# A fused attention and feed-forward kernel: a new order, new buffer slots and new queues for all its instructions, and the query norms of one batch taken from a product

## The chip, the cores and the metric

The kernel runs on one core of one Trainium2 chip. A core has a matrix engine (TensorE, PE in the profile; its weight loads are the row PEld), VectorE (DVE), ScalarE (ACT), GpSimd (POOL) and SyncE (SP). They run side by side, each through its own instructions in order, and wait for each other by semaphores. DMAs are issued from the instruction streams of SP and ACT and share 16 DMA engines. The metric is the device time of one execution in microseconds, as the median of several runs. TensorE's clock is granted at one of two levels, 1.2 or 2.4 GHz; the profile gives the mean granted share.

## The reference

For 8 batches and 8 heads of width 64 there are 512 local positions and 32 global ones. Global queries see everything; a local query sees the 32 global keys and the local keys at most 32 positions away. The result of the attention, 4352 rows of 512, goes through a feed-forward part with a smooth activation:

```
s_g   = scale * q_g @ concat(k_g, k_l).T ;  out_g = softmax(s_g) @ concat(v_g, v_l)
s_ll  = where(|i - j| <= 32, scale * q_l @ k_l.T, -1e9)
out_l = softmax(concat(scale * q_l @ k_g.T, s_ll)) @ concat(v_g, v_l)
x     = concat(out_g, out_l) as (4352, 512)
h     = x @ w_in                                   # 512 -> 2048
g     = h if h >= 1, 0 if h <= -1, else (h+1)^2/4
out   = g @ w_out                                  # 2048 -> 512
```

## The kernel before

Values are kept as pairs of 16-bit numbers, a high part and the remainder (`split`, `halves`), so that a product is made of three 16-bit products. Before a tensor is split it is scaled by a power of two taken from its norm. The weights arrive as 64-bit numbers and are decoded on the chip in the first part of the run.

The work is cut into named steps, about 900 of them. For batch b: `Lk`, `Lq`, `Lv` load keys, queries and values from the input; `sk`, `sq`, `sv` find their scales; `pk`, `pq`, `pv` split tile by tile and, for keys and queries, turn the tile (`turn`: by TensorE and a copy in batch 0, by a transposing DMA afterwards); `sw` and `vw` copy turned queries and shifted values within the on-chip memory by DMA; `aq` makes the local scores, `aa` their softmax and its turn, `ab` the product with the values, `ax` the normalised result, its split and its turn into the operand of the feed-forward part; `ga` and `gb` are the global queries. For the weights: `Lw`, `wd`, `ws`, `wh` load, decode, scale and split w_in; `Lo`, `od`, `oh` do so for w_out; `cb` and `rp` form sums of weight blocks. The feed-forward part works on tiles of 256 rows, s = 0 to 15: `m` is the first product with the activation (`moe1` for tiles 0 and 1, `moe_f`, a seven-product form that also uses the sums of blocks, afterwards), `o` the second product and the store.

`scale_q` finds the scale of a batch's queries: in batch 0 in two calls (`sq0a` for query tiles 0 and 1, `sq0b` for tiles 2, 3 and the global queries), later in one. With `gramq` "a" each tile's squares are summed by one ScalarE instruction (`squares`); with "p" the tiles are multiplied with themselves on TensorE (`gram`), VectorE sums the diagonal, and one small product adds that over the partitions (`total`, `all_sum`).

What is done is written by `attention_moe`; when it is issued is written out by hand. `segments` (line numbers below) cuts every step into stretches, the instructions of one step that run on one engine without an inner dependence, and numbers them in the order of the steps. `ORDER` is a list of these numbers. `build` records the instructions twice and issues the stretches in that order, so each engine runs its own stretches as `ORDER` has them. `SLOTS` says which of the fixed buffers each new tile takes (38 of 2 KB per partition called "room", 6 called "twin", 8 PSUM banks, and small ones). `T["queues"]` says for each plain load or copy in turn whether SP ("s") or ACT ("a") issues it; a load issued by SP also waits for the fifth SP load before it (`AHEAD`). Transposing DMAs are all issued by SP. Other letters in `T` choose the engine of one kind of instruction: `casts` and `subs` for the two halves of a softmax tile, `glow` for the remainder of an activation tile, `lows` and `lowx` for the remainder of an attention result, `turns` for the copy behind a turn by TensorE in batch 0 (a ScalarE, v VectorE, p GpSimd).

Every instruction is issued from line 1348 and every DMA from lines 1351 and 1353, so the profile's groups are told apart by tiles: "room", "bank" (PSUM), "twin", "weights_w" and small ones.

Of the kernel before, what the change touches and what calls it, by code (L numbers as in the profile page):

```python
# [118 lines left out]
def plan(steps, tiles):  # L119

    sizes, line = segments(steps, tiles)
    order = [int(x) for x in ORDER.split()]
    assert sorted(order) == list(range(len(sizes)))
# [8 lines left out]
def attention_moe(nc, memory, q_l, k_l, v_l, q_g, k_g, v_g, w_in, w_out, out):  # L132
# [1137 lines left out]
    for _, _, fn, a in sorted(steps.values(), key=lambda x: x[:2]):  # L1270
# [8 lines left out]

SLOTS = {  # L1280
# [27 lines left out]
}  # L1308

T = dict(es="nnnn", gramq="aaaaaaaa", dg="vvvvvvaaaaavvav", sid="vvvvv", fast=2, grams="ppaaaaaa", sqs="maamaa", cb=200, cbs=5, lk0=4.19,  # L1310
         lq0=1.76, lv0=12, sk=12, sq=14, subs="ppppppvppvppvpppppppvpvppvppvppppvvvvvpppvppvppppvpppvvvpppvpvpp",
         glow="ppppvvpppvpppvppppvvppvppvpvvppvpppppvpvppvpppvvppppvvvppvvpvvvpppvpvvpvppppvppvppvpvpvpppppppvvpvpppppvppppvvvvpvppvpvvpppvppvvpppppppppppppppp",
         turns="aaaaaaaaaaavvvvvvvvaaaa", casts="aaaaaavvaaaavvvvvvvaavavaaavvvaaavvaaaaaavaavvvvvaaaavvaavavaaav",
         mags="aapapvpaappvppppppapapaaaaapaaaa", lowx="ppppppppvpvvpppvppppppvpvpppvpvvvppvvpvppppvpvpp",
         lows="ppppvpppppppvpppppvpvpppvpppvpvp", halves="aaaaaahaabacadacceccacdbidffcbdf", shifts="vavvaaavvvvaaavvvvvavvvvvaaavvvv",
         splits="wpvpwwpvwwvpvvvw", att=1.35, s0=60, s1=100, s2=254.09, wd0=4, wds=2.06, wd8=19.2, wdt=1.9, wh=1.5, whs=1.4, od=58.2,
         ods=2.2, oh=0.7, ohs=0.92, e0=25.78, e1=70, e2=120, e3=156, w0=24.7, w1=24.34, w2=25.15, w3=25.51, z1=18.29, lq1=24, lv2=24.36,
         sv=24.5, sqb=35.02, pk2=20.4, pk3=30, pk4=45.8, pq2=28.03, pq4=44, pv=35.24, pvs=0.33, lw=0.54, lo=32.46, los=2.12, mk=8, mks=2,
         queues="saasasaaassaassaaaaasassaaaaaaassasaaaasasaasassasasssasssasssasssssasssaasssssssaaaaasassaaaasassssssaaaaaassasaasaassasaasasssssssssaasssassssssasssaasssssassaasaaaasassasasssaasssssaaassasssssaasassaasssaassasssssassasaassasasaasssaaaasasaasasssssasaassaaasssssasasaasaassaaasssasssssaaaasssssaassssssaassaaaasaasasaaaaassssasasssaassassassaassaaaassasaassssssaasasssssasasassaasaaasssaaaassassaasssasssaassassassssasassaasasasasaassaasssassasssssaasasaaaasssaasssssaassasassasaassssaassassasasassaaassssssassasaaaaasssaassasasassasaassssasasassaassssaasasaaasassaasssasass")
# [70 lines left out]
```

## Time and profile before

| | |
|---|---|
| median of 3 runs | 925.06 us (923.33 to 927.4) |
| the profiled execution | 925.07 us |
| its span (first to last instruction) | 923.0 us |
| TensorE busy, share of the span | 845.0 us, 92% |
| VectorE busy | 744.2 us, 81% |
| ScalarE busy | 643.9 us, 70% |
| GpSimd busy | 311.1 us, 34% |
| mean granted clock of TensorE | 0.993 |

A busy time is the union of an engine's instructions, so it takes in waits between matmuls that overlap in their pipeline. The idle time of an engine is put down to the engine or DMA that released it. Idle time costs only where that engine is the one all others wait for.

### The profile page before, as it was taken

The numbers are of one execution on the slowest core, as the hardware profiler recorded it, in microseconds if no ns is written. First come the engines' busy times: TensorE is split into PE (matmuls) and PEld (weight loads), VectorE is DVE, ScalarE is ACT, GpSimd is POOL, SyncE is SP. The second block draws the span as 40 slices with busy tenths as digits, with TensorE's granted clock in tenths as the row PEclk, the third lists the DMA queues.
The fourth block names the chain that finished last, engine by engine and source line by source line (L and its number), as shares of the span: only waits on it lengthen the run. The fifth ranks groups of instructions, "written<-read, shape, count | busy, mean of one in ns | idle before, by whom it ended". The sixth has DMA issues, their size and how long they took to land.

```text
span 923.0 us, 34948 instructions
## 1 busy us (share of the span) xinstructions
PE 845.0 (92%) x14380; PEld 613.3 (66%) x14380; DVE 744.2 (81%) x2008; ACT 643.9 (70%) x1592; POOL 311.1 (34%) x350
## 2 busy tenths in 40 slices
PE   1487889999999999899899998999999999999998
PEld 1354787557866766767586857668677768686953
DVE  3889999998889986799878888787979859867661
ACT  2698797878768877578668776778588658654530
POOL 3425354614232333232413212422435052324140
PEclk9989999999999999999999999999999999999999
DMA  9988896599989999999997979999987894772101
GB/s 237 243 219 202 190 187 116 121 198 165 177 150 179 175 171 164 155 173 167 166 178 110 163 163 172 163 151 192 178 160 139 159 147 90 129 128 36 26 19 51
DMA packets 379711, 140.96 MB, mean 153 GB/s; under 512 B 348576, under 2 KB 357792, under 8 KB 379552
## 3 DMA queue, kind: packets, MB, share of 16 engines
q1 hardware_dynamic: 305968, 98.94, 64.8%
q10 hardware_dynamic: 73584, 39.80, 19.0%
q8 instruction: 112, 1.84, 0.9%
q14 instruction: 47, 0.39, 0.2%
HBM read 49.81 MB, written 8.91 MB: 64 GB/s over the span
## 4 chain that ended last, share of the span: by engine, by line
PE 48%; DVE 19%; DMA 17%; ACT 7%; issue 4%; POOL 2%; ACTq 1%; SPq 1%; DVEq 0%; POOLq 0%
PE bank L1348 48%; DVE room L1348 11%; DMA room<-room 8%; ACT room L1348 5%; DVE bank L1348 3%; POOL room L1348 2%; DMA room<-in_q_l_dram 2%; DMA room<-in_v_g_dram 2%; DMA weights_w<-in_moe_w_in_dram 1%; DVE weights_w L1348 1%; ACT junk_junka L1348 1%; DMA room<-in_k_g_dram 1%; ACTq L1351 1%; DMA out_dram<-room 1%; DMA pg_gpt<-const_pgb 1%
## 5 line engine op out<-in xcount | busy, mean ns | idle before, releaser
L1348 POOL TENSOR_TENSOR room<-room,room 128x512 f16<-128x512 f32 (+3 forms) x228 | 245.8, 1090 | 505.8 <-ACT room L1348 379.9
L1348 PEld LDWEIGHTS <-room 128*32 128x32 f16 (+3 forms) x7560 | 249.4, 97 | 238.8 <-issue 33.5
L1348 PE MATMUL bank<-weights_w,room 128*128 128x512 f16 x1632 | 367.5, 379 | 3.5 <-issue 1.1
L1348 PEld LDWEIGHTS <-weights_w 128*128 128x128 f16 (+1 forms) x3968 | 220.1, 98 | 32.4 <-DVE weights_w L1348 13.9
L1348 PE MATMUL bank<-room,weights_w 128*128 128x128 f16 (+1 forms) x3840 | 221.4, 216 | 8.5 <-ACT room L1348 2.6
L1348 ACT CAST room<-room 128x512 f16<-128x512 f32 (+1 forms) x245 | 140.2, 587 | 69.9 <-DVE room L1348 48.4
L1348 PE MATMUL bank<-room,twin 128*128 128x128 f16 (+1 forms) x2304 | 132.6, 217 | 9.2 <-DMA room<-room 6.4
L1348 PEld LDWEIGHTS <-twin 128*128 128x128 f16 x2304 | 125.5, 98 | 16.1 <-DMA room<-room 7.3
L1348 ACT ACTIVATE room<-room,small_nb 128x128 f32<-128x128 f32 x256 | 100.6, 394 | 26.5 <-DVE small_nb L1348 21.7
L1348 ACT ACTIVATE room<-bank,batch_small_ms 128x512 f32<-128x512 f32 (+1 forms) x112 | 83.1, 749 | 31.6 <-DVE bank L1348 11.9
L1348 DVE SCALAR_TENSOR_TENSOR bank<-bank,batch_small_ms,room 128x512 f32<-128x512 f32 (+1 forms) x112 | 80.3, 722 | 21.8 <-ACT room L1348 21.7
L1348 ACT ACTIVATE junk_junka<-room 128x512 f16<-128x512 f32 (+2 forms) x124 | 77.4, 624 | 25.6 <-DMA room<-in_q_l_dram 6.7
L1348 ACT COPY room<-bank 128x512 f32<-128x512 f32 (+2 forms) x104 | 60.1, 585 | 41.8 <-PE bank L1348 38.9
L1348 DVE TENSOR_TENSOR room<-room,room 128x512 f16<-128x512 f32 (+1 forms) x90 | 69.8, 779 | 16.9 <-ACT room L1348 16.5
L1348 DVE CUSTOM_DVE_ANT_0 room<-bank,const_mask,batch_small_q 128x128 f32<-128x128 f32 x256 | 74.0, 345 | 7.4 <-PE bank L1348 4.3
L1348 DVE SCALAR_TENSOR_TENSOR room<-room,batch_small_ms,bank 128x512 f32<-128x512 f32 (+1 forms) x112 | 78.8, 712 | 1.0
L1348 DVE TENSOR_TENSOR bank<-bank,room 128x512 f32<-128x512 f32 (+1 forms) x64 | 42.0, 659 | 19.9 <-PE bank L1348 16.1
L1348 DVE SCALAR_TENSOR_TENSOR room<-room,batch_small_ms,room 128x512 f32<-128x512 f32 (+1 forms) x64 | 49.5, 775 | 6.1 <-ACT room L1348 5.8
L1348 ACT ACTIVATION_READ_ACCUMULATOR room<-room,small_nb 128x1 f32 x256 | 48.3, 189 | 0.0
L1348 DVE TENSOR_SCALAR room<-bank,batch_small_ms 128x512 f32<-128x512 f32 x34 | 25.3, 745 | 25.3 <-PE bank L1348 24.6
L1348 DVE SCALAR_TENSOR_TENSOR room<-room,batch_small_sk,room 128x512 f16<-128x512 f32 (+1 forms) x46 | 37.9, 829 | 5.3 <-ACT room L1348 4.1
L1348 PE MATMUL bank<-keys_kt,room 128*32 128x128 f16 x2048 | 37.8, 223 | 2.6 <-DMA room<-room 1.8
(168 smaller groups left out, 893.1 us busy)
## 6 DMA issues: line engine op xcount, KB each, us to landing
room<-room SPq DMA_DIRECT2D x87, 128.0 KB, 4.4
room<-room ACTq DMA_DIRECT2D x57, 128.0 KB, 4.2
weights_w<-in_moe_w_in_dram ACTq DMA_DIRECT2D x21, 256.0 KB, 5.2
room<-in_q_l_dram SPq DMA_DIRECT2D x20, 256.0 KB, 5.3
twin<-in_moe_w_out_dram ACTq DMA_DIRECT2D x17, 256.0 KB, 4.8
out_dram<-room SPq DMA_DIRECT2D x17, 256.0 KB, 4.3
room<-in_v_l_dram SPq DMA_DIRECT2D x22, 192.0 KB, 3.8
room<-in_k_l_dram SPq DMA_DIRECT2D x21, 192.0 KB, 4.8
```

Source lines behind the costliest of these rows:

```text
L1348: getattr(getattr(tc.nc, engine), op)(*a, **k)
L1351: r = (tc.nc.scalar if queue[n] == "a" else tc.nc.sync).dma_start(*a)
```

## The change

- All stretches are put in a new order, and all buffers get new slots. `ORDER` has 4417 numbers in place of 4411.
- Of the 576 letters of `queues`, 293 differ (s 323, a 253 become s 326, a 250).
- Engines: `subs` 31 letters differ (VectorE's share 20 becomes 23), `glow` 63 (48 becomes 49), `casts` 27 (27 becomes 30), `lowx` 15 (15 becomes 16), `lows` 9 (7 becomes 8), `turns` 12 (8 stays 8).
- `gramq` is "p" for batch 0: its query norms come from `total`. The code of `total` was there and unused.
- The small tile lists change to match (`small.tr` is new, `small.asx` has 16 entries in place of 14).

The function that takes another path, unchanged in text:

```
    def total(o, tiles, name):
        t = gram(tiles, f"gr{name}")
        tr = sm.tile([P, 1], F32, tag="tr", name=f"tr{name}")
        nc.vector.tensor_tensor_reduce(out=t, in0=t, in1=ident, scale=1.0, scalar=0.0, op0=ALU.mult, op1=ALU.add, accum_out=tr)
        all_sum(o, tr, name)
```

The diff, cut: the first numbers of each long list, and the letters that the prediction speaks of.

```diff
-ORDER = ("9 8 61 62 63 40 193 64 0 298 66 41 38 39 3 29 27 37 30 28 33 32 34 31 2 76 77 78 79 80 81 82 83 84
...
+ORDER = ("12 13 3 2 99 100 101 102 103 0 85 66 47 46 211 304 58 185 5 231 29 212 305 186 306 299 104 307 308 300
...
 SLOTS = {
-    "room": "11 12 4 3 6 5 2 1 0 28 34 11 22 13 10 15 20 29 17 33 14 19 23 36 31 37 24 20 26 16 21 32 25 16 17
...
+    "room": "0 1 18 5 13 19 14 7 24 1 22 9 23 9 32 11 17 21 21 36 34 35 10 2 26 25 29 19 32 3 6 31 28 2 3 16 5
...
+    "small.tr": "0 0",
+    "small.asx": "0 0 1 1 0 1 0 1 1 0 1 0 1 0 1 0",
...
-T = dict(es="nnnn", gramq="aaaaaaaa", dg="vvvvvvaaaaavvav", sid="vvvvv", fast=2, grams="ppaaaaaa", sqs="maamaa", cb=200, cbs=5, lk0=4.19,
+T = dict(es="nnnn", gramq="paaaaaaa", dg="vvvvvvaaaaavvav", sid="vvvvv", fast=2, grams="ppaaaaaa", sqs="maamaa", cb=200, cbs=5, lk0=4.19,
...
-         turns="aaaaaaaaaaavvvvvvvvaaaa", casts="aaaaaavvaaaavvvvvvvaavavaaavvvaaavvaaaaaavaavvvvvaaaavvaavavaaav",
+         turns="aaavavvvvaaaaavaaavavaa", casts="avaaaaavaavaavavvvavvavaavaavavavvaaaaaaavvvavvvavvaaavvvvavavav",
...
```

(In `turns` the letters stand for key tiles 0 to 5, query tiles 0 to 4, the eight softmax tiles and the four results of batch 0.)

## Rows read from the trace of the kernel before

**Rows 1.** The page's first part: busy us (share), count, of each engine.

```profile
PE 845.0 (92%) x14380; PEld 613.3 (66%) x14380; DVE 744.2 (81%) x2008; ACT 643.9 (70%) x1592; POOL 311.1 (34%) x350
```

**Rows 2.** Busy time by stage: start:end length, engines, granted clock, DMA share, GB/s.

```profile
0.00:46.14 46.14, 14.02 (x196) 11.62 (x197) 28.12 (x67) 20.48 (x37) 19.77 (x51) 1.00 1.06 240
46.14:207.63 161.49, 142.42 (x2361) 103.53 (x2361) 153.26 (x455) 135.23 (x334) 68.25 (x67) 0.97 0.83 176
207.63:899.73 692.10, 669.64 (x11755) 489.77 (x11743) 559.68 (x1485) 487.61 (x1224) 223.12 (x232) 1.00 0.86 145
899.73:923.00 23.27, 18.87 (x88) 8.35 (x86) 3.15 (x5) 0.62 (x1) 0.00 (x0) 1.00 0.16 53
```

**Rows 3.** TensorE's waits in 207.63 to 899.73: us, times, longest.

```profile
PE bank L1348 <- DMA room<-room: 12.8, 11, 3.8
PE bank L1348 <- DVE room L1348: 3.3, 5, 1.2
```

**Rows 4.** Timeline of the start: us, duration, engine, instruction, count, idle before it.

```profile
10.49 1.04 PE L1348 MATMUL bank<-room 128*128 128x128 bf16 x8 [10.49 <-DMA room<-in_k_l_dram]
13.54 1.86 PE L1348 MATMUL bank<-room 128*128 128x128 bf16 x16 [2.02 <-DMA room<-in_k_g_dram]
...
15.44 0.29 DVE L1348 TENSOR_REDUCE small_amk<-bank 128x1 f32<-128x128 f32 x1 [7.86 <-PE bank L1348]
...
17.34 0.16 DVE L1348 RECIPROCAL batch_small_sk<-batch_small_sk 128x1 f32<-128x1 f32 x1
...
19.72 1.11 POOL L1348 TENSOR_SCALAR room<-room,batch_small_sk 128x512 f32<-128x512 f32 x1
...
40.69 1.04 PE L1348 MATMUL bank<-keys_kt,room 128*32 128x128 f16 x32
```

**Rows 5.** Groups by shape, whole run: count, busy us, mean ns, idle before.

```profile
L1348 POOL TENSOR_TENSOR room<-room,room 128x512 f16<-128x512 f32 x157 | 192.3, 1236 | 432.9 <-ACT room L1348 329.3 <-DVE room L1348 35.8 <-DMA room<-room 19.7
...
L1348 ACT CAST room<-room 128x512 f16<-128x512 f32 x215 | 129.3, 613 | 64.2 <-DVE room L1348 43.0 <-PE bank L1348 4.2 <-DMA room<-room 4.1
...
L1348 DVE TENSOR_TENSOR room<-room,room 128x512 f16<-128x512 f32 x85 | 67.0, 793 | 15.5 <-ACT room L1348 15.1
L1348 ACT ACTIVATE junk_junka<-room 128x512 f16<-128x512 f32 x102 | 63.7, 624 | 18.9 <-DMA room<-in_q_l_dram 6.7 <-DMA room<-in_k_g_dram 5.0 <-DMA room<-in_k_l_dram 2.3
...
L1348 ACT ACTIVATION_READ_ACCUMULATOR junk_junka<-room 128x1 f32 x102 | 19.2, 188 | 0.0
...
L1348 POOL TENSOR_TENSOR room<-room,room 128x256 f16<-128x256 f32 x25 | 18.4, 745 | 63.8 <-ACT room L1348 50.6 <-DVE room L1348 13.3
...
L1348 DVE CAST room<-room 128x512 f16<-128x512 f32 x27 | 12.6, 469 | 5.3 <-ACT room L1348 5.0
```

**Rows 6.** Groups by shape in 46.14 to 207.63: the copies behind turns.

```profile
L1348 DVE COPY room<-bank 128x1024 f16<-128x1024 f16 x8 | 5.3, 679 | 0.0
...
L1348 ACT COPY room<-bank 128x1024 f16<-128x1024 f16 x6 | 5.9, 990 | 0.0
```

**Rows 7.** DMA issues: engine, kind, count, KB each, median us to landing.

```profile
room<-room SPq DMA_DIRECT2D x87, 128.0 KB, 4.4
...
room<-room SPq DMA_TRANSPOSE x140, 4.4
```

**Rows 8.** TensorE's timeline: three of its waits for DMAs.

```profile
374.88 5.46 PE L1348 MATMUL bank<-room,twin 128*128 128x128 f16 x72 [3.83 <-DMA room<-room]
441.65 1.92 PE L1348 MATMUL bank<-keys_kt,room 128*32 128x128 f16 x124 [1.79 <-DMA room<-room]
453.12 0.55 PE L1348 MATMUL bank<-room,room 128*32 128x64 f16 x48 [1.59 <-DMA room<-room]
```

**Rows 9.** TensorE by stretch behind the first of them: busy, granted clock, DMA share, GB/s.

```profile
374.00:376.00 2.00, 1.12 (x11) 0.54 1.28 146
376.00:378.00 2.00, 2.00 (x25) 0.61 0.76 223
378.00:380.00 2.00, 2.00 (x39) 1.00 0.57 129
```

**Rows 10.** Timeline of the end: last products, last VectorE instruction.

```profile
889.73 28.87 PE L1348 MATMUL bank<-weights_w,room 128*128 128x512 f16 x133
...
918.64 0.75 DVE L1348 TENSOR_SCALAR room<-bank,batch_small_ms 128x512 f32<-128x512 f32 x1 [1.84 <-PE bank L1348]
```

**Rows 11.** TensorE's timeline: one run of short products, for their spacing.

```profile
446.10 1.50 PE L1348 MATMUL bank<-room,weights_w 128*128 128x128 f16 x24
```

More of the change, by code (lines that the diff above doesn't have):

```diff
@@ L1308 @@
 }
-T = dict(es="nnnn", gramq="aaaaaaaa", dg="vvvvvvaaaaavvav", sid="vvvvv", fast=2, grams="ppaaaaaa", sqs="maamaa", cb=200, cbs=5, lk0=4.19,
-         lq0=1.76, lv0=12, sk=12, sq=14, subs="ppppppvppvppvpppppppvpvppvppvppppvvvvvpppvppvppppvpppvvvpppvpvpp",
-         glow="ppppvvpppvpppvppppvvppvppvpvvppvpppppvpvppvpppvvppppvvvppvvpvvvpppvpvvpvppppvppvppvpvpvpppppppvvpvpppppvppppvvvvpvppvpvvpppvppvvpppppppppppppppp",
-         turns="aaaaaaaaaaavvvvvvvvaaaa", casts="aaaaaavvaaaavvvvvvvaavavaaavvvaaavvaaaaaavaavvvvvaaaavvaavavaaav",
-         mags="aapapvpaappvppppppapapaaaaapaaaa", lowx="ppppppppvpvvpppvppppppvpvpppvpvvvppvvpvppppvpvpp",
-         lows="ppppvpppppppvpppppvpvpppvpppvpvp", halves="aaaaaahaabacadacceccacdbidffcbdf", shifts="vavvaaavvvvaaavvvvvavvvvvaaavvvv",
+T = dict(es="nnnn", gramq="paaaaaaa", dg="vvvvvvaaaaavvav", sid="vvvvv", fast=2, grams="ppaaaaaa", sqs="maamaa", cb=200, cbs=5, lk0=4.19,
+         lq0=1.76, lv0=12, sk=12, sq=14, subs="vpppppppvpppvvppvpppvvpvpvvppvppppvppppvvvvvpvvpppppvpppppvppvpv",
+         glow="ppppvppppvppppppvppvpvpvpvppppvvvpvppvpppvppppvpvpvpppvvpppvppvvvpppvvvpvvpvppvppppppvppppvvpvppvpvvvppvppppvppvvpvppvvpppvpvvvvpppppppppppppppp",
+         turns="aaavavvvvaaaaavaaavavaa", casts="avaaaaavaavaavavvvavvavaavaavavavvaaaaaaavvvavvvavvaaavvvvavavav",
+         mags="aapapvpaappvppppppapapaaaaapaaaa", lowx="ppppppppvpppvvvvpppvppvpvpppvpppvpvvpvppvpvvpppp",
+         lows="vpppppppvpppvpppvpppppvpppvpvpvp", halves="aaaaaahaabacadacceccacdbidffcbdf", shifts="vavvaaavvvvaaavvvvvavvvvvaaavvvv",
          splits="wpvpwwpvwwvpvvvw", att=1.35, s0=60, s1=100, s2=254.09, wd0=4, wds=2.06, wd8=19.2, wdt=1.9, wh=1.5, whs=1.4, od=58.2,
@@ L1318 @@
          sv=24.5, sqb=35.02, pk2=20.4, pk3=30, pk4=45.8, pq2=28.03, pq4=44, pv=35.24, pvs=0.33, lw=0.54, lo=32.46, los=2.12, mk=8, mks=2,
-         queues="saasasaaassaassaaaaasassaaaaaaassasaaaasasaasassasasssasssasssasssssasssaasssssssaaaaasassaaaasassssssaaaaaassasaasaassasaasasssssssssaasssassssssasssaasssssassaasaaaasassasasssaasssssaaassasssssaasassaasssaassasssssassasaassasasaasssaaaasasaasasssssasaassaaasssssasasaasaassaaasssasssssaaaasssssaassssssaassaaaasaasasaaaaassssasasssaassassassaassaaaassasaassssssaasasssssasasassaasaaasssaaaassassaasssasssaassassassssasassaasasasasaassaasssassasssssaasasaaaasssaasssssaassasassasaassssaassassasasassaaassssssassasaaaaasssaassasasassasaassssasasassaassssaasasaaasassaasssasass")
+         queues="asassssasssaaaaaaassasasasasasaasaaaassasaassssssssasaaassssssssaaaaasassasssssaasssassaasssasassssssassasasasssasassaasasassaaassaassssaasaasaasasaasaasssssssasssssassssaasaasssassasasssassassssaassasssaassssasassassasasassasasaaasassasssasaaaaaasaaaaaassaassasaasasaasassaaasssaaaasasasassssasasasassssassaaasaaaaaaaassssssssaasaaasasasassaasssassaasssssaassssssaassasaasssaaaaasssaaassassssassasssaaaassaasssasaasasassasaasaaasaassassssassaaasasssssaassssssaaasssssassssssasasssssssssaassssaaaasssasssaaaaaaaasssassassasasasassssssssasasssassaasaasaasasassaaasasassssaaaass")
 KEYS = 2
```

2 lines of the change are left out of this document (1 added, 1 removed), and 21 rows, old and new, of the table SLOTS.

## The prediction, made before the change was timed

> **What bounds the kernel now.** I read the page's busy times first: TensorE is busy for 92% of the span, no other engine for more than 81% [rows 1]. An average over 923 us says little, so the table by stage comes next [rows 2]. It shows three regimes. In the first 46.14 us TensorE works 14.0 us and the DMA engines are full (share 1.06, 240 GB/s): the start waits for data. From 46.14 to 207.63 TensorE works 142.4 of 161.5 us while VectorE works 153.3, or 95%; there VectorE is the tightest. From 207.63 to 899.73 TensorE is busy 669.6 of 692.1 us and VectorE only 81%; TensorE is the bound and idles 22.5 us in all. The last 23 us are its final products and the store. Idle TensorE is all that a new order can give back: 32.1 + 19.1 + 22.5 + 4.4 = 78 us, of which the first term hangs on the loads and the last on the final store.
>
> The waits of TensorE in the third stage come third: 12.8 of the 22.5 us are for DMAs within the chip (turned or shifted tiles), 11 times, the longest 3.8 us [rows 3]. Three single ones show where [rows 8]; the longest also costs clock: behind it the granted share is 0.54 and 0.61 for two windows of 2 us and then 1.00 again [rows 9], that is (0.46 + 0.39) x 2 = 1.7 us at half clock.
>
> The sum is made against the profiled execution, 925.07 us, of which 2.07 lie outside the span; the median of the runs shown is 925.06, so nothing has to be shifted.
>
> **How the two orders can be compared without running them.** `ORDER` numbers stretches of named steps. Step times, and so the numbering, are the same in both versions but for the norms: in `sq0a` and again in `sq0b`, `total` has five stretches where two squares stood, so a new number is the old one up to `sq0a`, 3 more behind it and 6 more behind `sq0b` (4411 + 6 = 4417, as the lists have it). So every number has a name on either side, and I can count what stands ahead of what. Where I weigh a distance, a 128x512 product counts 0.22 us (133 in 28.87 us [rows 10]) and a 128x128 one 0.06 us (24 in 1.50 us [rows 11]), and a VectorE instruction the mean of its kind. These are distances within an order, not times.
>
> **Part 1, the norms by a product.** Removed: four squares on ScalarE, each 0.624 + 0.188 us [rows 5], 3.2 us. Added: 16 small products (eight take 1.04 us [rows 4]) and two single ones, 2.1 us of TensorE; and on VectorE two sums over a diagonal, two casts and two copies, about 2 x 0.29 + 4 x 0.16 = 1.2 us by the nearest rows [rows 4]. TensorE runs nothing before 10.49 us and is idle two thirds of the first stage, so the products cost 0 while they stay there; if they had to queue behind other work they would cost their 2.1 us. ScalarE's 3.2 us are worth 0 in that stage too (20.5 of 46.1 us busy).
>
> **Part 2, the start.** Queries now load first, weights between, and the last piece of batch 0's keys is issued behind 6.1 MB of loads; before, behind 2.0 MB. The keys' products started by 13.54 us [rows 4], so 2.0 MB took 11.7 us (174 GB/s); at the stage's 240 GB/s 6.1 MB take 25.4 us from 1.8 us on, which puts the last keys at 27 us. From there the shortest chain to the first scores is: products 1.9 and the scale's small operations 2.1 (15.44 to 17.50), then key tile 1 by GpSimd (1.11 scaling, 0.61 cast, 1.24 subtraction), turn 8 x 0.06, copy 0.99 [rows 4 to 6, 11]: 8.5 us, so the first scores could start at 35.5 us. They start at 40.69 us now [rows 4]. So the late keys need not delay anything. VectorE is the check: 31.1 us of its work stood ahead of the fourth score product, 34.4 us stand there now, but of that 15.2 us are placed ahead of the key norms where 2.2 us were, and can be done while the keys load. Later the two orders need the same VectorE work per TensorE work (138.2 and 138.7 us ahead of the point where TensorE has done 80 us, 203.3 and 201.0 at 150). I take 0 for the loads, with bounds of -5.2 (scores at 35.5) and +4.7 (keys at 174 GB/s: 35 + 1.8 + 8.5 = 45.4).
>
> **Part 3, the engine letters in the second stage.** VectorE copied all eight softmax turns of batch 0 there, 0.679 us each [rows 6]; now two, and one of the results' turns: -4.1 + 0.7. The five other copies moved to VectorE are of the keys and queries, in the first stage, where it idles. `glow` of tiles 0 to 3 goes from 11 to 9 on VectorE (-1.6 at 0.793 [rows 5]), `lowx` of tile 3 from 2 to 0 (-1.0, half size, taken as 0.5 each), `casts` of batch 1 from 4 to 3 (-0.5), `subs` of batch 1 from 2 to 3 (+0.8). Sum -5.7 us of 153.3. ScalarE takes five copies of 0.99 and a cast of 0.6; it has 26 us free there. How much of 5.7 arrives depends on whether VectorE's waits fill again; bounds -5.7 and 0, and I take -3. Over the whole run, by the same means (three whole `subs`, one `glow`, one `lows`, half a `lowx`, three `casts`), VectorE gains 5.9 + 1.2 us of work, nothing where it is 81% busy and TensorE the bound; with that cover gone it would be up to 5.9 us.
>
> One thing could turn this part round. Four subtractions go from VectorE to GpSimd (two whole, two of half size). If VectorE had to stand still while GpSimd runs them, they would cost it 2 x 1.24 + 2 x 0.75 = 4.0 us [rows 5] where I credit 2.6; the part would come to -5.7 + 2.6 + 4.0 = +0.9, halved as above +0.5, and the sum 3.5 us later. In the stage the two were recorded busy for 153.3 + 68.3 us of 161.5 [rows 2], so at least 60 us overlap; a blocked span may count as busy, so this does not settle it, and I keep the 3.5 us as a rival. The Trainium skill, "SBUF — State Buffer", section "SBUF: two separate sides", states such a rule: GpSimd and a VectorE instruction with two on-chip inputs shut each other out for the whole instruction. By that rule the sum is 922.5, by the overlap of the rows 919; I go by the rows.
>
> **Part 4, the steady stage.** A DMA lands 4.4 us after issue [rows 7]. Of the transposing DMAs placed beyond 150 us of TensorE work, 30 had their first product less than 4.4 us of TensorE work behind them; in the new order 20. Of the copies 14; now 19. Together 44 become 39. Below 3 us it is 26 against 27. So the slack is wider for the turns, not for the copies, and by the counts 5/44 of 12.8 + 1.7 us goes, 1.6 us. By place: the 3.83 us wait (tile 5's sums behind the turn of batch 2's last result) had 2.8 to 3.8 us and gets 8.1 to 9.5; the 1.59 us wait (last quarter of batch 3) 8.1, now 12.0; the 1.79 us wait (queries 1 of batch 4) 2.7, now 0, which may grow to 4.4 [rows 8]. That is -3.8 - 1.7 - 1.6 + 2.6 = -4.5. I take -3, between the two, with bounds of -14.5 (all of it) and +8.8 (two new full landings). Changed queue letters I price at 0: both queues stay as full (326 and 250 against 323 and 253).
>
> **Part 5, the end.** The last products are again those of tiles 14 and 15, followed by a VectorE instruction and a store [rows 10]: 0, bounds -1 and +2 (two more stores wait near the end).
>
> Sum: 925.07 + 0 + 0 - 3 - 3 + 0 = 919.
>
> **Rivals.** (a) *No change*: what the wider turns give, the closer copies take, and VectorE's 5.7 us refill: 925. For it: 26 against 27 below 3 us. Against it: the longest wait is one that gets wider. (b) *Slower, by the keys*: they load at 174 GB/s behind 6.1 MB, first scores at 45.4 us in place of 40.69, and since VectorE is 95% busy behind that nothing is made up; the two sw/vw hand-overs at 0 distance add up to 2.6: 925 + 4.7 + 2.6 = 932. It decides from keys later than 40.69 - 8.5 = 32.2 us, or below 200 GB/s. For it: the same kind of load had 174. Against: the stage's mean is 240, and queries are ready earlier. (c) *Much faster*: all of part 3, all DMA waits of the steady stage: 925 - 5.7 - 14.5 = 905. For it: slack at the places where it waited. Against: the unchanged counts. (d) *GpSimd holds VectorE*: 922.5, by 60 us of overlap unlikely to cost it all.
>
> **Chances.** The forecast (913 to 920) 0.35, (c) 0.15, (a) 0.22, (d) 0.05, (b) 0.23. What a measurement of this kernel can tell from no change is about 0.5%, 4.6 us: faster is below 920.4, 0.35 + 0.15 = 0.50; same 0.22 + 0.05 = 0.27; slower, above 929.7, 0.23. The range runs from 905, the end of (c), to 931, just short of (b), and leaves 0.1 on either side; the likeliest case alone spans 913 to 920.
>
> **What would show it.** Right: key products at about 27 us and first scores by 41; VectorE's busy time in 46 to 207 us down by 3 to 6 us with TensorE's up; the DMA waits of the steady stage near 10 us with none at tile 5's sums. Wrong: first scores beyond 45 us (b); a new wait of 3 us or more with a clock near 0.5 behind it; VectorE spans longer beside GpSimd's (d). The forecast fails as a whole if the third stage's idle time changes by more than 9 us either way.

## The result and the profile after

The changed kernel takes 917.75 us as the median of 20 runs, against 927.98 us for the kernel before, measured beside it in 20 runs. The ratio is 0.9892, with a 95% interval of 0.9861 to 0.9922: 1.1% faster, some 10 us. The forecast was 919.0 us, a ratio of 0.9934 on its own base of 925.07.

The first profiled execution of the changed kernel (924.27 us) was granted less clock than any other run of it (mean 0.971), so what follows is read from a second profiled execution, of 912.69 us; its span is 911.0 us.

The page's busy times after; the row before is [rows 1]:

```profile
PE 843.1 (93%) x14398; PEld 612.4 (67%) x14398; DVE 737.5 (81%) x2025; ACT 638.0 (70%) x1581; POOL 300.0 (33%) x344
```

TensorE's span is its busy time and its idle time. Before, 923.0 = 845.0 + 78.0; after, 911.0 = 843.1 + 67.9. So 10.1 of the 12.0 us between the two executions (their medians differ by 10) are idle time that is gone; the other 1.9 us are busy time, although the change adds 18 products. Where the idle time went is in the table by stage, with the second and the third stage cut once more. First the kernel before, then the changed one (columns as in [rows 2]):

```profile
46.14:102.00 55.86, 46.10 (x726) 30.58 (x725) 52.89 (x181) 50.20 (x132) 21.73 (x25) 0.91 0.82 206
102.00:207.63 105.63, 96.32 (x1639) 72.95 (x1638) 100.37 (x275) 85.02 (x203) 46.51 (x42) 1.00 0.83 161
207.63:420.00 212.37, 203.66 (x3544) 147.83 (x3532) 177.90 (x486) 159.34 (x404) 72.73 (x76) 0.99 1.04 167
420.00:899.73 479.73, 465.98 (x8215) 341.94 (x8212) 381.78 (x1000) 328.27 (x821) 150.39 (x156) 1.00 0.78 135
```

```profile
0.00:46.14 46.14, 17.50 (x174) 14.18 (x175) 30.51 (x69) 16.40 (x25) 17.95 (x49) 0.85 1.05 228
46.14:102.00 55.86, 40.72 (x717) 26.29 (x715) 53.07 (x189) 49.55 (x133) 17.62 (x21) 0.91 0.95 223
102.00:207.63 105.63, 103.57 (x1808) 78.90 (x1806) 98.14 (x288) 89.41 (x214) 55.21 (x55) 1.00 0.91 166
207.63:420.00 212.37, 207.51 (x3602) 153.79 (x3600) 182.67 (x494) 166.93 (x419) 63.72 (x65) 1.00 1.00 169
420.00:899.73 479.73, 466.47 (x8078) 336.09 (x8076) 370.18 (x984) 315.71 (x792) 145.54 (x155) 1.00 0.79 132
899.73:911.00 11.27, 7.33 (x34) 3.14 (x32) 2.91 (x4) 0.00 (x0) 0.00 (x0) 0.95 0.31 118
```

Length less TensorE's busy time is its idle time:

| us of the span | idle before | idle after | difference |
|---|---|---|---|
| 0 to 46.14 | 32.1 | 28.6 | -3.5 |
| 46.14 to 102 | 9.8 | 15.1 | +5.4 |
| 102 to 207.63 | 9.3 | 2.1 | -7.3 |
| 207.63 to 420 | 8.7 | 4.9 | -3.9 |
| 420 to 899.73 | 13.8 | 13.3 | -0.5 |
| the end | 4.4 | 3.9 | -0.5 |

The gain stands in two places: between 102 and 207.63 us, where TensorE now hardly waits at all, and between 207.63 and 420 us. The first row is not a gain of its own: of the 3.5 us by which TensorE is busier there, 2.8 are the new norm products. From 46 to 102 us the changed kernel even waits more; its first scores come later (44.16 against 40.69 us, below). Behind 420 us the two run alike.

TensorE's waits from 207.63 to 899.73 us after (columns as in [rows 3]):

```profile
PE bank L1349 <- issue: 7.4, 5, 2.5
PE bank L1349 <- DVE room L1349: 5.8, 8, 2.3
PE bank L1349 <- DMA room<-room: 2.7, 4, 0.8
```

The 12.8 us for on-chip DMAs have become 2.7, and the longest 0.8. Other traces bear this out: the first profile of the changed kernel has 3.4 us of them and run 7, with the same order, 4.4, while runs 4 and 6 with the old order have 15.0 and 12.1. Against these 10.1 us stand 7.8 of others: waits for VectorE's tiles went from 3.3 to 5.8 us, and gaps that the trace gives no reason for ("issue") from 2.1 to 7.4. Whether it is the same time passed on is not shown; run 4, whose time does not differ from the kernel before's, has 9.4 us of such gaps. The stage's idle time is down by 4.4 us, from 22.5 to 18.1.

The start of the changed kernel, by the timeline (columns as in [rows 4]):

```profile
26.09 2.83 PE L1349 MATMUL bank<-room 128*128 128x128 bf16 x24
...
30.53 0.28 DVE L1349 TENSOR_REDUCE small_amk<-bank 128x1 f32<-128x128 f32 x1
...
33.97 0.15 DVE L1349 RECIPROCAL batch_small_sk<-batch_small_sk 128x1 f32<-128x1 f32 x1
...
37.81 4.02 DVE L1349 SCALAR_TENSOR_TENSOR room<-room,batch_small_sk,room 128x512 f16<-128x512 f32 x3
38.42 1.01 ACT L1349 COPY keys_kt<-bank 128x1024 f16<-128x1024 f16 x1 [0.40 <-PE bank L1349]
...
44.16 1.04 PE L1349 MATMUL bank<-keys_kt,room 128*32 128x128 f16 x32
```

The keys' products start at 26.09 us, and the first scores at 44.16, where they started at 40.69 before [rows 4].

### The profile page after: what moved, and what is told of

It reads as the page before. It is cut to its first block, busy times and chain, and to the rows that moved or that the text cites. A ratio compares the mean times of both kernels' runs of the same rounds, so it can differ in the third digit from the quotient of the medians.

```text
span 922.5 us, 35007 instructions
## 1 busy us (share of the span) xinstructions
PE 851.5 (92%) x14398; PEld 619.4 (67%) x14398; DVE 738.2 (80%) x2025; ACT 638.8 (69%) x1581; POOL 300.5 (33%) x344
## 4 chain that ended last, share of the span: by engine, by line
PE 53%; ACT 4%; DVE 4%; DMA 3%; issue 2%; ACTq 0%; POOL 0%; SPq 0%; DVEq 0%
PE bank L1349 53%; ACT room L1349 3%; DVE room L1349 3%; DMA room<-room 2%; ACT junk_junka L1349 1%; DMA keys_kt<-room 1%; DMA room<-in_k_g_dram 0%; DVE batch_small_q L1349 0%; DMA room<-in_v_g_dram 0%; ACT const_gpf L1349 0%; DVE bank L1349 0%; ACTq L1352 0%; POOL room L1349 0%; DVE batch_small_ms L1349 0%; DVE const_pgb L1349 0%
## 5 line engine op out<-in xcount | busy, mean ns | idle before, releaser
L1349 PEld LDWEIGHTS <-room 128*32 128x32 f16 (+3 forms) x7576 | 254.4, 99 | 240.7 <-issue 38.4
L1349 POOL TENSOR_TENSOR room<-room,room 128x512 f16<-128x512 f32 (+3 forms) x222 | 234.9, 1068 | 531.4 <-ACT room L1349 387.4
L1349 ACT ACTIVATE junk_junka<-room 128x512 f16<-128x512 f32 (+2 forms) x120 | 75.1, 626 | 13.3 <-DMA room<-in_v_g_dram 4.6
L1349 ACT COPY room<-bank 128x512 f32<-128x512 f32 (+2 forms) x106 | 62.6, 595 | 31.3 <-PE bank L1349 24.3
L1349 DVE SCALAR_TENSOR_TENSOR room<-room,batch_small_sv,room 128x512 f16<-128x512 f32 (+1 forms) x47 | 38.8, 832 | 4.8 <-ACT room L1349 4.5
```

What stands on the lines that cost most here:

```text
L1349: getattr(getattr(tc.nc, engine), op)(*a, **k)
```

## The experiments

My theory (theory 1 in the expectations) was the prediction's: the second stage gains because VectorE is relieved, the steady stage because products stand farther behind the DMAs that feed them, and each gives a few microseconds on its own. The rivals put all of the gain in one of the two stages, or say that order, letters and buffers are worth something only together. "Planned" buffers are those that `SLOTS` of the kernel before or of the changed one lists for its own order. Each run was timed in five rounds beside the kernel before; ratios below 1 are faster than that kernel.

**1. The changed kernel again.** No edit.

> The changed kernel once more, for a second profile. All theories: ratio to the kernel before 0.986 to 0.992, as measured. In its profile, theory 1 (mine: both the VectorE-bound second stage and the steady stage give a few us each) expects TensorE's waits for on-chip DMAs beyond 207.63 us near 10 us against 12.8 before. Theory 2 (the steady stage gives all) expects them under 4 us and idle TensorE beyond 207.63 us below 15 us against 22.5. Theory 3 (the first 207 us give all) expects TensorE to be ahead by some 10 us of work at 207 us.

Measured: 0.9869 (0.9813 to 0.9925). The DMA waits are 2.7 us, as theory 2 (all from the steady stage) had them, but the idle time beyond 207.63 us is 22.1 us with the end's, against 26.9: less than 5 us. At 207.63 us TensorE had done the same scores as before and, beyond them, 12 products of 128x512, 96 of 128x64 and 11 of 128x256. At 0.22 us [rows 10], 0.01 (96 of them take 0.98 us) and 0.11 (half of a 128x512) that is 4.8 us ahead. So of 12.0 us in these two executions some 5 were there by 207.63 us and some 7 came behind: theory 1's split at twice its sizes, though not its DMA waits near 10 us. The split is rough. In the first profile of the changed kernel TensorE was 1.5 us ahead at 207.63 us (11 products of 128x512 more, 8 of 128x256 fewer), in run 7, with the same order, 2.0 us (12 more, 6 fewer).

**2 and 3. The order cut in two.** One run has the new order, letters, queues and buffers for the first 1263 stretches and the old ones behind, the other the reverse. At the cut some 17 stretches stand on the other side, so some 100 tiles find their buffer taken and get another free one.

```diff
-ORDER = ("... 1280 1281 1267 1268 1269 1321 1388 1389 1203 962 ...
+ORDER = ("... 1280 1281 1267 1167 1357 1353 1352 1356 1365 1784 ...
```

> The first 1263 stretches (about 207 us) in the new order with the new slots, queues and engine letters, all that is left in the old order with the old ones. Theory 1: half of the gain, 0.993 to 0.997. Theory 2 (all from the steady stage): 0.998 to 1.002. Theory 3 (all from the head): 0.987 to 0.991. If head and rest work only together: above 1.0.

> The reverse: the first 1263 stretches in the old order with the old slots, queues and letters (the norms by the product), the rest as in the changed kernel. Theory 1: 0.993 to 0.997. Theory 2: 0.987 to 0.991. Theory 3: 0.998 to 1.002. If the two halves are independent, the gains of this run and of the one with the new head add up to that of the whole change, about 1.1%.

Measured: 1.0344 (1.0286 to 1.0403) and 1.0448 (1.0384 to 1.0511). No theory had this but the last words of the first expectation. The table of the first of the two by stretch shows what each half did:

```profile
46.14:102.00 55.86, 43.21 (x719) 28.07 (x718) 52.24 (x189) 49.30 (x133) 17.76 (x21) 0.88 0.96 224
102.00:207.63 105.63, 104.02 (x1811) 79.07 (x1808) 97.53 (x290) 89.58 (x214) 55.55 (x56) 1.00 0.85 167
...
207.63:420.00 212.37, 183.64 (x3105) 136.44 (x3104) 146.48 (x400) 137.17 (x345) 59.24 (x59) 0.94 0.82 142
```

Up to the cut it runs as the changed kernel does (idle 1.6 us in 102 to 207.63, against 2.1): that gain belongs to the first 1263 stretches, with their buffers and letters, and does not need the rest. Behind the cut, 28.7 us of 212.4 are idle. With the old head, the idle time of 102 to 207.63 us is back at 10.5 us.

**4. The norms alone.** The kernel before, with the ten stretches of the product where the squares stood.

```diff
-T = dict(es="nnnn", gramq="aaaaaaaa", ...
+T = dict(es="nnnn", gramq="paaaaaaa", ...
```

> The kernel before with one change: batch 0's query norms by the product, its ten new stretches standing where the squares stood. All theories: 0.998 to 1.002, since TensorE idles two thirds of the first stage. If the small products queue behind late loads, 1.002 to 1.005.

Measured: 1.0021 (0.9986 to 1.0057): no difference that can be told, as expected.

**5 and 6. The engine letters.** The 26 letters of the first 1263 stretches, put back in the changed kernel, and put into the kernel before; the turns as an example:

```diff
-         turns="aaavavvvvaaaaavaaavavaa",
+         turns="aaaaaaaaaaavvvvvvvvaaaa",
```

> The changed kernel with the 26 engine letters of its first 1263 stretches (some 207 us) put back: five subs, two glow, twelve turns, five casts, two lows; order, slots and queues new. Theory 1 (the letters relieve VectorE in the second stage by 5.7 us, of which 3 arrive): 3 us slower than the changed kernel, ratio to before 0.990 to 0.995, and VectorE busy 3 to 6 us longer in 46.14 to 207.63. Rival (the gain of the head comes from the order, the letters are worth nothing): 0.985 to 0.990. Second rival (an order is worth only what its own letters make of it): above 0.997.

> The kernel before with the same 26 letters as the changed kernel has them, all else old. Theory 1: 0.994 to 1.000, about 0.997, VectorE busy 3 to 6 us less in 46.14 to 207.63. Rival (the order alone): 0.999 to 1.003. Second rival (letters and order fit each other): 1.004 or more, with new waits for ScalarE's copies behind turns.

Measured: 0.9967 (0.9938 to 0.9997) and 1.0073 (1.0038 to 1.0108). The same letters are worth 0.75% in the new order (0.9967 less 0.9892, some 7 us) and cost 0.7% in the old one. The stages of the second of these two runs:

```profile
46.14:207.63 161.49, 143.34 (x2360) 103.60 (x2361) 146.34 (x435) 133.47 (x322) 68.87 (x68) 0.92 0.79 169
207.63:899.73 692.10, 666.20 (x11757) 490.17 (x11755) 559.05 (x1497) 490.18 (x1236) 219.53 (x229) 0.99 0.86 147
```

VectorE's busy time in the second stage fell from 153.26 to 146.34 us, but not by the letters alone. Of the 20 instructions fewer (435 against 455 [rows 2]) the letters are some seven, 4.7 us by the prediction's prices; the others had not been reached. By 207.63 us TensorE had done 71 products fewer than in the kernel before (2486 against 2557), among them 12 of 128x512, 24 of 128x256 and 32 scores: some 6 us of its work.

The loss starts at the first scores. VectorE's instructions start within 0.1 us of those before up to 35 us. Then VectorE copies three turned tiles of queries and keys that ScalarE copied before (the first at 35.64 us), and its first masked scores come 2.3 us later. Before, and in run 6:

```profile
42.28 0.35 DVE L1348 CUSTOM_DVE_ANT_0 room<-bank,const_mask,batch_small_q 128x128 f32<-128x128 f32 x1 [0.15 <-DVE batch_small_q L1348]
```

```profile
41.24 0.68 DVE L1348 COPY room<-bank 128x1024 f16<-128x1024 f16 x1
41.85 0.68 DVE L1348 COPY keys_kt<-bank 128x1024 f16<-128x1024 f16 x1
...
44.62 0.35 DVE L1348 CUSTOM_DVE_ANT_0 room<-bank,const_mask,batch_small_q 128x128 f32<-128x128 f32 x1 [0.15 <-PE bank L1348]
```

In run 5 the five copies of keys and queries are back on ScalarE, and none of the other letters acts ahead of the first scores. These start at 46.55 us, where three executions with the new letters have 43.42, 44.16 and 45.03, and at 207.63 us TensorE is not ahead of the kernel before (2 products of 128x512 more, 8 of 128x256 fewer). The waits between 102 and 207.63 us stay away with the old letters all the same (3.7 us idle).

In the third stage, which these letters do not touch, the idle time is 25.9 us in run 6, within what two other executions of the old order show (22.5 before, 30.2 in run 4), and 25.1 in run 5, above three of the new order (17.9 to 20.9). The second rival holds, though not by waits for ScalarE's copies: a letter is worth what the order around it makes of it.

**7. The queues.** The changed kernel with the old letters, 293 of 576.

```diff
-         queues="asassssasssaaaaaaassasasasasas...
+         queues="saasasaaassaassaaaaasassaaaaaa...
```

> The changed kernel with the old queue letter for every load and copy (293 of 576 differ), all else new. Theory 1 (priced at 0 in the prediction): 0.985 to 0.992. Rival (a transfer on the wrong queue stands behind a waiting instruction): above 0.996, with more waits of TensorE for on-chip DMAs.

Measured: 0.9845 (0.9808 to 0.9881). The new queues are worth nothing that can be seen; whether the old ones are a little better stays open, since this interval and that of the changed kernel overlap.

**8. Other buffers, by the simplest rule.**

```diff
 SLOTS = {
-    "room": "0 1 18 5 13 19 14 7 24 1 22 9 23 9 32 11 17 21 21 ...
+    "room": "0 1 19 5 14 20 15 7 26 10 23 0 24 9 34 12 18 25 22 ...
```

> The changed kernel with each new tile in the buffer that has been free longest in the order (1605 of 2121 tiles change place), all else new. Theory 1 (the slots were priced at nothing): 0.985 to 0.992. Rival (the slots decide when a write may start, as the two mixed orders with some 100 tiles in other buffers suggest, which lost 3.4% and 4.5%): above 1.01, with TensorE waiting for ScalarE and VectorE copies that wait for a buffer.

Measured: 1.0559 (1.0506 to 1.0612), so buffers alone cost 6.7% of the changed kernel's time. ScalarE's largest waits for DMAs, over the whole run, in the changed kernel and in this one:

```profile
ACT room L1349 <- DMA room<-room: 17.1, 14, 3.6
```

```profile
ACT room L1349 <- DMA room<-room: 62.7, 33, 5.0
```

One reading is that a buffer that stood free for long in the order need not be free, because a DMA is still reading it. Runs 9 to 11 test that.

**9 to 11. Other buffers, with landings allowed for.** A buffer counts as free only 6 us behind the last DMA on it, in the changed kernel, in the kernel before and in the first of the two cut orders.

```diff
 SLOTS = {
-    "room": "0 1 18 5 13 19 14 7 24 1 22 9 23 9 32 11 17 21 21 ...
+    "room": "37 36 18 32 23 17 22 30 11 24 14 25 13 28 3 25 19 ...
```

> The changed kernel with all large buffers chosen anew, by one rule: a buffer counts as free 6 us after the issue of the last DMA that reads or writes it and 1 to 2 us after the last use by another engine (estimated times: TensorE work ahead in the order), and the one free longest is taken. Theory A (buffers released late by a DMA made the run with the longest-free rule slow): the loss goes, 0.980 to 0.995, and ScalarE waits for on-chip DMAs less than the 17.1 us of the changed kernel (62.7 with the longest-free rule). By this count (DMA-released buffers short of 6 us, in summed us: before 208, changed 187, longest-free 306, this 68) it could even be faster than the changed kernel. Rival B (a choice other than the planned one loses because it makes more waits between engines, whatever the DMAs): above 1.02.

> The kernel before with its buffers chosen by the same rule (short of 6 us: 92 in place of 208), order, letters and queues old. Theory A: 0.985 to 1.003; at 0.990 or lower the slots alone would be worth as much as the whole change. Rival B: above 1.02. If theory 1 holds (the gain is in the order, 6 us by 207 us and 6 us behind), this run is at 0.997 to 1.003 and not at 0.989.

> The mixed order with the new first 1263 stretches and the old rest, its buffers now chosen by the same rule (short of 6 us: 72 in place of 244). Theory A: the 3.4% loss was the buffers' and goes, to 0.990 to 1.000; with half of the gain in the head, 0.995. Rival B: stays above 1.02. Rival C (the seam itself, some 17 stretches that stand out of place, costs it): stays at 1.02 to 1.035 although ScalarE's waits for on-chip DMAs fall.

Measured: 1.0366 (1.0319 to 1.0413), 1.0518 (1.0474 to 1.0562) and 1.0654 (1.0611 to 1.0697). ScalarE's waits in the first of them:

```profile
ACT room L1349 <- DMA room<-room: 11.4, 9, 3.9
```

The waits that the rule was made for fell below the changed kernel's, and the time rose all the same. What rose is the time in which SP stood at a DMA until a product had released the buffer, here beyond 207.63 us, in the changed kernel and then in this one (line 1354 issues the turns, line 1352 the plain transfers):

```profile
SPq L1354 <- PE bank L1349: 15.6, 14, 3.1
SPq L1352 <- PE bank L1349: 13.5, 18, 2.4
```

```profile
SPq L1354 <- PE bank L1349: 45.6, 23, 7.5
SPq L1352 <- PE bank L1349: 37.8, 25, 4.9
```

ScalarE's waits for DMAs fell in run 10 too, from 10.1 us before to 8.7. Theory A falls, and rival B holds. Run 11 was to tell the buffers from the seam; with its buffers worse than the planned ones it can't, and the cost of the seam itself stays open.

**12. More distance behind the DMAs, in the kernel before.** In the steady stage alone, products are moved behind others and a few turns ahead; the first stretches that move:

```diff
-ORDER = ("... 1263 1313 1314 1242 1287 1199 1348 951 1266 1374 ...
+ORDER = ("... 1263 1242 1287 1199 1348 951 1266 1374 1375 1376 ...
```

> The kernel before with its steady stage reordered so that products stand farther behind the turn or copy that feeds them: of the DMAs whose first product has less than 4.4 us of TensorE work behind the issue, 42 become 10 (14 become 2 below 2 us). 107 of 656 TensorE stretches, 43 of ScalarE's, 30 of VectorE's and 10 of SP's stand elsewhere, by at most some us; seven tiles exchange two buffers; letters, queues and the first 1263 stretches are old. Theory 1 (waits for on-chip DMAs are worth their own time, part 4 of the prediction): those waits fall from 12.8 us to 5 or less, the third stage's idle time from 22.5 to 13 to 17, ratio 0.988 to 0.995. Rival 1 (what the DMAs no longer hold up, other waits do): the DMA waits fall as far, the idle time stays at 20 to 25, ratio 0.997 to 1.003. Rival 2 (a planned order loses by any departure, as in the four runs with other buffers and the two with other letters): idle time above 26, ratio above 1.005.

Measured: 1.0385 (1.0352 to 1.0418). TensorE's waits from 207.63 to 899.73 us:

```profile
PE bank L1348 <- DVE room L1348: 17.0, 14, 3.5
PE bank L1348 <- DVE small_nb L1348: 8.8, 4, 3.2
PE bank L1348 <- ACT room L1348: 6.5, 10, 1.4
PE bank L1348 <- DMA room<-room: 6.1, 5, 1.9
```

The waits for on-chip DMAs were halved, from 12.8 to 6.1 us, and those for VectorE's tiles grew from 3.3 to 17.0 us and for its small results from 1.0 to 8.8. The idle time of the stage is 47.4 us where 22.5 was (692.10 less 644.68). Rival 2 holds, far beyond its bound. By the page the whole run is 961.4 = 856.9 + 104.5: 26.5 us of idle time, and 11.9 us of products at a lower clock (0.980 on the mean against 0.993). So beside 26.5 us more of waiting stand 11.9 us more of busy time. The run does not show that distance to a DMA is worth nothing: the moves that gave it also brought TensorE to VectorE's tiles before they were done.

No run beat the changed kernel by more than its interval.

## Why the prediction was right, and where it was not

The time was right and the direction too; by the sum's own terms:

**The norms, 0.** Right: 1.0021 alone, and all eighteen products lie ahead of 12 us (from 4.70 to 11.57), where TensorE has nothing else to do.

**The start, 0 with bounds of -5.2 and +4.7.** Right as a sum, wrong in its chain. The keys' products start at 26.09 us, 27 was forecast, so the load rate was taken rightly. But from there to the first scores I counted 8.5 us, the bare durations, and it took 18.1: VectorE reaches the first reduction 1.6 us after the products, ends the scale 3.6 us later, and then has three key remainders to do for 4.02 us. The chain left out that VectorE has other work between its links, and the sign "first scores by 41" failed. First scores at 44.16 us are nearly rival (b)'s 45.4, but (b)'s price did not follow: its claim that nothing is made up behind the scores is refuted by 102 to 207.63 us.

**Part 3, -3 with bounds of -5.7 and 0.** The place was right and the size within its bounds: 1.5 to 4.8 us by 207.63, in three executions of the new order. The reason given is refuted as a mechanism by itself. VectorE's busy time in the stage fell by 2.1 us only (153.26 to 151.21, 3 to 6 were forecast), with 476 instructions in place of 455, and the letters alone made the kernel 0.7% slower. In the changed kernel the same letters are needed for the gain. Two steps fail. The two subtractions of `lowx` (1.0 of the 5.7 us) are not in the stage: they stand behind the first 1263 stretches in both orders. And the five copies of keys and queries were put at nothing, "in the first stage, where it idles"; in the old order they put VectorE's first masked scores 2.3 us later (run 6), and with the new order they bring the first scores forward by 1.5 to 3.1 us (run 5). I priced the letters as a term that can be added, and they are none without their order.

**Rival (d), GpSimd holds VectorE.** GpSimd's 128x512 instructions took 1222 ns where they took 1236. No run isolates this rival. Two of its four subtractions are those of `lowx`, behind the stage, and run 6 moved only one more to GpSimd than away from it (68 of its instructions in the stage against 67). The Trainium skill, "SBUF — State Buffer", section "SBUF: two separate sides", has the later of two such instructions, one of GpSimd and one of VectorE with two on-chip inputs, blocked whole. The rows do not show that price.

**Part 4, -3 with bounds of -14.5 and +8.8.** Right in place, too small in size. The wait at tile 5's sums, 3.83 us and the 1.7 us of half clock behind it [rows 8, 9], is gone; no DMA wait above 0.8 us is left (1.4 in the first profile), and their sum is 2.7 us, where I had it near 10. Some 7 us of the gain of these two executions lie behind 207.63 us: 4.8 are idle time, most of it ahead of 420, the rest less busy time. No new wait of 3 us or more came up (the longest is 2.5), and the third stage's idle time changed by 4.4 us, inside the 9 that I had set as the mark of failure. But my measure, the TensorE work between a DMA and its first product, fell only from 44 to 39 short ones and could not have told this: the waits fell to a fifth. And run 12, which improved that measure from 42 short ones to 10 and kept letters, queues and all but seven buffers, lost 3.85%; it had to move 107 of TensorE's stretches for it. The measure leaves out when a DMA's source is done, when its buffer is released and what stands ahead of it in SP's queue. None of these is isolated here. The turn behind the 3.83 us wait takes a buffer that `gb2` reads in some of its 72 products, and does so in the new order too. In the trace of the kernel before these products end at 366.75 us, and the turn is issued 1.2 us later:

```profile
364.47 2.28 PE L1348 MATMUL bank<-pg_gpt,room 128*128 128x64 f16 x72
...
367.96 1.27 SPq L1353 DMA_TRANSPOSE room<-room  x1
```

Its product starts at 374.88 us [rows 8], 6.9 us behind the issue, where the median landing is 4.4 [rows 7].

**Queue letters, 0.** Right: 0.9845 with the old ones.

**Buffers.** The prediction gave them no term. No run separates the new buffers from the new order, so whether that was right for this change stays open: both kernels have planned buffers. As a general price it is wrong by far, 5% to 7% (runs 8 to 10, each against the kernel whose buffers were replaced).

So the sum came out near because places and signs of its two terms were right, and because 6 us of forecast gain against 10 measured is within half a per cent of the whole. That 5.4 us more of idle time from 46 to 102 us, where the sum had nothing, was more than made up by the 7.3 behind it is luck. It was not right as an account of causes that can be added. That TensorE runs from 102 to 207.63 us almost without waiting comes with the new order and its buffers: 2.1 us are idle there, 3.7 with the old letters, 3.3 with the old queues, but 10.6 with the buffers of run 9, and 9.2 in the old order with the new letters. What feature of the order does it was not found.

## What to carry to other kernels

In a kernel whose order, buffers and engines are planned together, a forecast by parts gives the places and rough sizes, but a part taken out of the plan is no longer worth its term: here runs 9, 10 and 12 lowered the waits they aimed at and still lost 3.7% to 5.2% against the kernel before. Change such a plan as a whole and measure it as a whole. For a chain through a busy engine, add the work that stands between its links, not only the links. And ask of each moment, not of the stage's mean, whether an engine idles: VectorE was busy for 28.1 of the first 46.14 us [rows 2], and yet three copies at the end of them put its first masked scores off by 2.3 us.

## What was not expected of the hardware

Buffers of the same size and kind, in a kernel with the same order and the same engines, decide over 6.7% of the time (run 8). And more idle time went with slower products: in the run with the most of it (the third of runs 9 to 11, 125.9 us) the products' busy time was 872.2 us at a mean granted share of 0.957, in the run with the norms alone (84.2 us idle) 847.9 at 0.988, so that 24.3 us more of busy time stand beside 41.7 us more of waiting. The tie is loose: run 10, with 121.3 us idle, has 861.8 us busy at 0.981, and the first profile of the changed kernel, with 71.0 us idle, 851.5 at 0.971.
